# Pooled attention and a mixture of four experts on one core: another head, folds spread over slots, scores on row halves

## The chip, the cores and the metric

The kernel runs on one core of a Trainium2 chip. The core has a matrix engine (PE, TensorE) with its weight loads (PEld), a vector engine (DVE), a scalar engine (ACT), GpSimd (POOL) and a queue engine (SP). Each takes its own instructions in the order of the program; they wait for each other through semaphores. Loads are issued by POOL (queue q0 in the profile, "software_dynamic") or by SP (q1, "hardware_dynamic") and run on 16 DMA engines. The metric is the device time of one launch in microseconds (us); less is better.

## The reference

```python
k_p = k.reshape(B, H, Sp, 8, D).mean(axis=3)          # B, H, S, D = 8, 8, 576, 64; Sp = 72
v_p = v.reshape(B, H, Sp, 8, D).mean(axis=3)
scores = q @ k_p.T / 8                                 # per batch and head: 576 x 72
attn = softmax(scores)
x = (attn @ v_p), heads side by side                   # 4608 tokens x 512
p = domain_probs / domain_probs.sum(-1)                # 4608 x 4
out = sum over e of p[:, e] * (relu(x @ w1[e]) @ w2[e])  # w1: 512 x 1024, w2: 1024 x 512, e = 0..3
```

Keys and values are means over 8 neighbouring tokens, so each head has 72 keys. Inputs and output are float32; the kernel's products are in bfloat16.

## The kernel before

**Tiles.** The 4608 tokens are 36 tiles of 128, in 9 groups of 4 (512 tokens). A batch has 576 tokens, so tiles 4, 13, 22 and 31 lie over two batches and do their attention in two halves of 64 tokens. A step `s` is one group with one expert, 36 steps in all. `up` computes 128 of the 1024 hidden units for a whole group: 4 products of 128x128 weights with 512 columns, then relu on ACT. `down` takes one tile through w2 in 8 products of 512 columns; `collect` scales the result by the tile's probability and adds it up on DVE; the last expert's sum is stored. Up and down products, 2272 of 512 columns, are most of the work of PE.

**Attention of a tile.** `turn_q` transposes the queries (128 x 512) into `qT`; `scores` multiplies them with `kT`, the transposed key sums; `less_max` takes the maximum off on DVE; `expo` is on ACT; `turn_e` transposes the exponents; `context` multiplies with `vblk`, the value sums spread into blocks per head; `divide` is on DVE; `turn_x` transposes the result into `xT`, which `up` reads. In `kpad` each key sum stands in the columns of its head's parity, the other 64 columns being zero through `mask_k`; one product of 128 rows thus gives the scores of a pair of heads (144 columns). For tiles 0 to 7 the transpositions are products with an identity followed by a copy; from tile 8 on (`DT`) they are DMA transpositions issued by SP.

**Sums of keys and values.** `prep_k` and `prep_v` fold the 8 tokens of a mean on DVE, 4 + 2 + 1, all at once in the place where they are called; `kraw` and `vraw` have two buffers each, so the load of batch b + 2 waits for the folds of batch b.

**The head** (lines 516 to 567) computes group 0 with expert 0, tile by tile, before the regular steps start. The keys of batch 0 (`k0`, float32) come through SP in two parts of 256 rows and one of 64, the queries of the first 512 tokens through POOL as one load (`qg`), which DVE copies out tile by tile (`split_q`).

**The regular steps.** Each step has 12 slots. Two slots of three hold one `up` of the *next* step, the third a `down` and `collect` of this one. `plan` attaches the attention's functions to slots by number: step s, slot i is s * 12 + i. `plan_tile` sets a tile's order by `lead`, `late` and `last`, the slots between turned queries and scores, exponents and context, and transposed result and first use. A tile's `load_q` for the tile four later stands one slot behind `turn_q`. `plan_batch` places a batch's folds and the loads of the batch after next. Engines run their instructions in the order in which these calls are made: a slot's own product first, then what the plan has put there, in the order of planning.

**The loads** are issued by POOL in program order, at most eight under way, each issue behind the landing of the one eight before. The weights of all experts (16.8 MB in float32) come in the first 64 us, between queries, keys and values.

## Time and profile before

| | us |
|---|---|
| median of three runs (573.11 to 574.27) | 573.2 |
| the profiled execution | 575.8 |
| its span | 574.1 |
| PE busy | 541.6 |
| DVE / ACT / POOL busy | 259.8 / 209.3 / 62.8 |
| first full-width up product starts | 48.35 |
| one up (4 x 512 columns) / one down (8 x 512) | 0.86 / 1.73 |

The profile is of one execution. Its lines give an engine, an operation, the tiles that it writes and reads, how often, its busy time, and the idle time ahead of it with what ended that. Matmuls are pipelined: a single product lasts longer (379 ns for 512 columns) than the distance to the next one (216 ns). The granted clock is the share of TensorE's full clock that its throttle let through.

### The profile page before, as it was taken

The numbers are of one execution on the slowest core, as the hardware profiler recorded it, in microseconds if no ns is written. First come the engines' busy times: TensorE is split into PE (matmuls) and PEld (weight loads), VectorE is DVE, ScalarE is ACT, GpSimd is POOL, SyncE is SP. The second block draws the span as 40 slices with busy tenths as digits, with TensorE's granted clock in tenths as the row PEclk, the third lists the DMA queues.
The fourth block names the chain that finished last, engine by engine and source line by source line (L and its number), as shares of the span: only waits on it lengthen the run. The fifth ranks groups of instructions, "written<-read, shape, count | busy, mean of one in ns | idle before, by whom it ended". The sixth has DMA issues, their size and how long they took to land.

```text
span 574.1 us, 7199 instructions
## 1 busy us (share of the span) xinstructions
PE 541.6 (94%) x2906; PEld 263.1 (46%) x2906; DVE 259.8 (45%) x441; ACT 209.3 (36%) x352; POOL 62.8 (11%) x90
## 2 busy tenths in 40 slices
PE   1689997999999999899999999999999999999997
PEld 1554443444444444444444444444444444444443
DVE  4534675444733447344644445544553344322223
ACT  1345453333333333333333333333333333333330
POOL 7233313000310002200130000000000000000000
PEclk9799998999999999999999999999999999999999
DMA  9999999321692116911792244312311221111002
GB/s 198 206 203 197 203 148 89 86 48 31 96 159 50 30 31 110 149 25 31 110 159 36 39 77 87 39 30 65 77 29 29 59 75 31 21 34 49 1 0 74
DMA packets 111233, 46.03 MB, mean 80 GB/s; under 512 B 88128, under 2 KB 105984, under 8 KB 111200
## 3 DMA queue, kind: packets, MB, share of 16 engines
q0 software_dynamic: 51888, 21.96, 32.3%
q1 hardware_dynamic: 59312, 23.62, 18.4%
q8 instruction: 23, 0.38, 0.3%
q14 instruction: 10, 0.08, 0.1%
HBM read 45.16 MB, written 9.44 MB: 95 GB/s over the span
## 4 chain that ended last, share of the span: by engine, by line
PE 89%; DMA 4%; DVE 4%; ACT 2%; issue 1%; SPq 0%; DVEq 0%
PE o_ps L439 41%; PE h_ps L407 40%; DMA eT<-ebuf 3%; PE x_ps L372 3%; PE sc L302 2%; PE h_ps L422 2%; DMA k<-in_k_dram 1%; DVE xr L381 1%; DVE acc L454 1%; PE xT_ps L286 1%; ACT xT L287 0%; DVE mx L313 0%; DVE d_sb L315 0%; DVE vblk L260 0%; PE v_ps L272 0%
## 5 line engine op out<-in xcount | busy, mean ns | idle before, releaser
L411 ACT ACTIVATE h_sb<-h_ps 128x512 bf16<-128x512 f32 x280 | 167.2, 597 | 308.2 <-PE h_ps L407 308.1
L439 PE MATMUL o_ps<-w,h_sb 128*128 128x512 bf16 x1152 | 274.3, 381 | 0.0
L407 PE MATMUL h_ps<-xT,w 128*128 128x512 bf16 x1120 | 265.0, 379 | 0.7 <-ACT xT L287 0.7
L454 DVE SCALAR_TENSOR_TENSOR acc<-o_ps,p_sb,acc 128x512 f32<-128x512 f32 x108 | 81.1, 751 | 210.2 <-PE o_ps L439 210.2
L439 PEld LDWEIGHTS <-h_sb 128*128 128x128 bf16 x1152 | 112.2, 98 | 133.3 <-issue 1.9
L407 PEld LDWEIGHTS <-w 128*128 128x128 bf16 x1120 | 108.0, 98 | 124.1 <-issue 1.5
L450 DVE TENSOR_SCALAR acc<-o_ps,p_sb 128x512 f32<-128x512 f32 x36 | 27.0, 751 | 70.4 <-PE o_ps L439 70.4
L109 POOL DMA_DIRECT2D qrow<-in_q_dram x36 | 30.4, 865 | 77.1 <-DMA qT<-qrow 66.7
L313 DVE TENSOR_REDUCE mx<-sc 128x8 f32<-128x576 f32 x36 | 27.0, 749 | 5.5 <-PE sc L302 5.5
L315 DVE TENSOR_TENSOR d_sb<-sc,mx 128x576 f32<-128x576 f32 x36 | 27.3, 758 | 1.4
L321 ACT ACTIVATE ebuf<-d_sb 128x576 bf16<-128x576 f32 x36 | 24.4, 678 | 4.2 <-DVE d_sb L315 4.2
L381 DVE TENSOR_TENSOR xr<-x_ps,rs 128x512 bf16<-128x512 f32 x36 | 24.6, 683 | 2.8 <-PE x_ps L372 2.7
L339 DVE TENSOR_REDUCE total<-ebuf 128x8 f32<-128x576 bf16 x32 | 23.8, 743 | 0.8 <-ACT ebuf L321 0.8
L372 PE MATMUL x_ps<-vblk,eT 128*128 128x192 bf16 (+5 forms) x200 | 20.4, 242 | 4.0 <-DMA eT<-ebuf 2.1
L82 POOL DMA_DIRECT2D kraw<-in_k_dram x7 | 5.3, 756 | 163.8 <-DVE k_sum L232 160.6
L372 PEld LDWEIGHTS <-eT 128*128 128x128 bf16 (+1 forms) x200 | 14.4, 100 | 14.8 <-ACT eT L287 3.5
L302 PE MATMUL sc<-kT,qT 128*128 128x144 bf16 (+1 forms) x160 | 15.8, 234 | 3.8 <-ACT qT L287 2.5
L302 PEld LDWEIGHTS <-qT 128*128 128x128 bf16 (+1 forms) x160 | 10.8, 102 | 7.3 <-ACT qT L287 4.8
L255 PE MATMUL kT_ps<-ident,kpad 128*128 128x128 bf16 x10 | 1.2, 264 | 11.7 <-DVE kpad L241 11.7
L82 POOL DMA_DIRECT2D vraw<-in_v_dram x8 | 6.2, 771 | 43.9 <-DVE v_sum L232 37.2
L286 PE MATMUL xT_ps<-ident,xr 128*128 128x128 bf16 x32 | 3.4, 232 | 7.4 <-DVE xr L381 7.4
L422 PE MATMUL h_ps<-xT,w 128*128 128x128 bf16 x128 | 9.5, 243 | 0.5 <-ACT xT L287 0.5
(61 smaller groups left out, 135.8 us busy)
## 6 DMA issues: line engine op xcount, KB each, us to landing
out_dram<-acc SPq DMA_DIRECT2D x36, 256.0 KB, 2.2
vraw<-in_v_dram POOLq DMA_DIRECT2D x8, 512.0 KB, 8.2
w<-in_moe_w_dram POOLq DMA_DIRECT2D x8, 512.0 KB, 16.7
w<-in_moe_w_dram POOLq DMA_DIRECT2D x4, 1024.0 KB, 17.3
kraw<-in_k_dram POOLq DMA_DIRECT2D x7, 512.0 KB, 6.9
qrow<-in_q_dram POOLq DMA_DIRECT2D x28, 128.0 KB, 9.3
k<-in_k_dram SPq DMA_DIRECT2D x2, 512.0 KB, 4.0
qg<-in_q_dram POOLq DMA_DIRECT2D x1, 512.0 KB, 9.1
```

The source lines that it names most:

```text
L109: nc.gpsimd.dma_start(out=qrow[t][at:at + n], in_=q[b][:, tok:tok + n, :].rearrange("h p d -> p h d"),)
L302: nc.tensor.matmul(sc[at:at + n, pair // 2, (pair % 2) * PW:(pair % 2 + 1) * PW], lhsT=qT[t][:, pair, at:at + n], rhs=flat[:, pair * PW:(p ...
L313: nc.vector.reduce_max(out=mx[:], in_=view, axis=AX.X)
L315: nc.vector.tensor_tensor(out=ds[t][:], in0=view, in1=mx[:].unsqueeze(3).to_broadcast([P, 2, 4, SP]), op=ALU.subtract,)
L321: nc.scalar.activation(out=ebuf[t % 2][:, 0:ROWS].rearrange("p (h j) -> p h j", j=SP), in_=ds.pop(t)[:].rearrange("p g h j -> p (g h) j"), ...
L372: nc.tensor.matmul(ps[at:at + n, (2 * i - 1 + z0) * D:(2 * i - 1 + z1) * D], lhsT=eT[t][:, i, at:at + n], rhs=vblk[b][:, i, z0:z1].rearran ...
L381: nc.vector.tensor_tensor(out=rows_x[t][:], in0=xps.pop(t)[:].rearrange("p (h d) -> p h d", d=D), in1=es.pop(t)[:].unsqueeze(2).to_broadca ...
L407: nc.tensor.matmul(ps[:], lhsT=w1_sb[e][:, kc, fb * P:(fb + 1) * P], rhs=xT[g][:, kc, :], start=(kc == 0), stop=(kc == KC - 1),)
L411: nc.scalar.activation(out=hs[s][:, fb, :], in_=ps[:], func=ACT.Relu)
L439: nc.tensor.matmul(ps[:], lhsT=hs[s][:, fb, i * P:(i + 1) * P], rhs=w2_sb[e][:, fb, :], start=(fb == 0), stop=(fb == FB - 1),)
L450: nc.vector.tensor_scalar_mul(out=accs[t][:], in0=ps[:], scalar1=p_sb[:, e, t:t + 1])
L454: nc.vector.scalar_tensor_tensor(out=accs[t][:], in0=ps[:], scalar=p_sb[:, e, t:t + 1], in1=accs[t][:], op0=ALU.mult, op1=ALU.add,)
```

## The change

The keys are laid out as 96 rows x 6 instead of 128 x 5 with a short last part. `last_k` writes each key sum twice, side by side, with no mask, so both halves of `kT`'s rows hold all keys; `scores` does one product a head with 64 rows, even heads on the upper half, odd heads on the lower, 72 columns each, into two banks. `k0` comes in three equal parts, each folded as it lands, and is transposed in two pieces. `qg` comes in two loads and is transposed straight from there. In the head, products of zeros (`warm`) fill waits of PE at the start, zero fills are done by ACT, and the four tiles' work is interleaved in another order. In the regular steps the folds of a batch are spread over three or four slots, those of keys and values apart; `late` is 11 instead of 9; a tile is begun two slots earlier (`base`). The loads of the batch after next follow each fold, so load_k(3) is now issued at slot 11 and load_v(3) at slot 16, where both were at slot 15; load_q(8) stays at slot 14, and the scores of tile 8 move from slot 29 to 27. The folds of batch 2 move from slots 23 (keys) and 29 (values) to 30 to 32 and 42 to 45.

```diff
-    PW = 2 * SP
+    KP = 96
+    KB = ROWS // KP
...
-    kraw = [raw.tile([P, NB, POOL * D], BF16, name=f"kraw{i}") for i in range(2)]
+    kraw = [raw.tile([KP, KB, POOL * D], BF16, name=f"kraw{i}") for i in range(2)]
...
     def load_k(b):
-        load_rows(nc.gpsimd, kraw[b % 2], k[b])
+        nc.gpsimd.dma_start(
+            out=kraw[b % 2][:], in_=rows_of(k[b]).rearrange("(i p) x -> p i x", p=KP)
+        )
...
-    k0 = raw.tile([P, NB, POOL * D], F32, name="k0")
-    load_rows(nc.sync, k0, k[0], ((0, 2), (2, 4)))
+    KPARTS = ((0, 2), (2, 4), (4, KB))
+    k0 = raw.tile([KP, KB, POOL * D], F32, name="k0")
+    for i0, i1 in KPARTS:
+        nc.sync.dma_start(
+            out=k0[:, i0:i1, :],
+            in_=rows_of(k[0])[i0 * KP:i1 * KP].rearrange("(i p) x -> p i x", p=KP),
+        )
...
-    qg = raw.tile([P, H, TPG, D], BF16, name="qg")
-    nc.gpsimd.dma_start(
-        out=qg[:], in_=q[0][:, 0:G, :].rearrange("h (p c) d -> p h c d", c=TPG)
-    )
+    qg = [raw.tile([P, H, 2, D], BF16, name=f"qg{i}") for i in range(2)]
...
+    def load_qg(i):
+        nc.gpsimd.dma_start(
+            out=qg[i][:],
+            in_=q[0][:, 0:G, :].rearrange("h (p c) d -> p h c d", c=TPG)[
+                :, :, 2 * i:2 * i + 2
+            ],
+        )
+
+    zero = const.tile([P, 2 * P], BF16, name="zero")
+    nc.vector.memset(zero[:], 0.0)
+    load_qg(0)
+    ident = const.tile([P, P], BF16, name="ident")
+    make_identity(nc, ident[:])
+    load_v(0)
...
-    ident = const.tile([P, P], BF16, name="ident")
-    make_identity(nc, ident[:])
-    load_v(0)
-    load_w1(0)
+    load_w1(0, (0,))
+    load_qg(1)
+    load_w1(0, (1,))
...
-    nc.vector.memset(k0[TAIL:P, NB - 1, :], 0.0)
-    for t in (*kraw, *vraw):
-        nc.vector.memset(t[TAIL:P, NB - 1, :], 0.0)
+    for t in vraw:
+        nc.scalar.memzero(t[TAIL:P, NB - 1, :])
     for t in ebuf:
-        nc.vector.memset(t[:, ROWS:NB * P], 0.0)
+        nc.scalar.memzero(t[:, ROWS:NB * P])
...
-    mask_k = const.tile([P, NB, 2, D], BF16, name="mask_k")
...
-    def last_fold(rows, nm):
-        s = prep.tile([P, NB, D], BF16, name=f"{nm}_sum")
-        nc.vector.tensor_add(out=s[:], in0=rows[:, :, 0:D], in1=rows[:, :, D:2 * D])
-        return s
-
-    def prep_k(b, rows=None, parts=((0, NB),)):
-        rows = kraw[b % 2] if rows is None else rows
-        for i0, i1 in parts:
-            fold(rows, i0, i1, 4, 2)
-        s = last_fold(rows, "k")
-        pad = prep.tile([P, NB, 2, D], BF16, name="kpad")
-        nc.vector.tensor_tensor(
-            out=pad[:], in0=s[:].unsqueeze(2).to_broadcast([P, NB, 2, D]),
-            in1=mask_k[:], op=ALU.mult,
-        )
-        pads[b] = pad
-
-    def prep_kT(b, by_dma=True):
-        kT[b] = prep.tile([P, NB, P], BF16, name="kT")
+    def last_k(b, rows, i0, i1):
+        if i0 == 0:
+            pads[b] = prep.tile([KP, KB, 2, D], BF16, name="kpad")
+        shape = [KP, i1 - i0, 2, D]
+        nc.vector.tensor_add(
+            out=pads[b][:, i0:i1],
+            in0=rows[:, i0:i1, 0:D].unsqueeze(2).to_broadcast(shape),
+            in1=rows[:, i0:i1, D:2 * D].unsqueeze(2).to_broadcast(shape),
+        )
+    def fold_k(b, n):
+        fold(kraw[b % 2], 0, KB, n)
+    def end_k(b):
+        last_k(b, kraw[b % 2], 0, KB)
+    def kT_tile(b):
+        kT[b] = prep.tile([P, KB, KP], BF16, name="kT")
+        return pads[b][:].rearrange("p i z d -> p (i z d)")
+    def turn_k(b):
+        flat = kT_tile(b)
+        nc.sync.dma_start_transpose(out=kT[b][:], in_=flat)
+    def turn_k_by_products(b, i0, i1, pool, tag):
+        if i0 == 0:
+            kT_tile(b)
         flat = pads[b][:].rearrange("p i z d -> p (i z d)")
-        if by_dma:
-            nc.sync.dma_start_transpose(out=kT[b][:], in_=flat)
-            return
-        ps = ps_t.tile([P, NB, P], BF16, tag="t", name="kT_ps")
-        for i in range(NB):
-            nc.tensor.transpose(ps[:, i, :], flat[:, i * P:(i + 1) * P], ident[:])
-        nc.scalar.copy(out=kT[b][:], in_=ps[:])
-
-    def spread_v(b, s):
+        ps = pool.tile([P, i1 - i0, KP], BF16, tag=tag, name="kT_ps")
+        for i in range(i0, i1):
+            nc.tensor.transpose(
+                ps[:, i - i0, :], flat[:, i * P:(i + 1) * P], ident[0:KP, 0:KP]
+            )
+        nc.scalar.copy(out=kT[b][:, i0:i1, :], in_=ps[:])
...
+    def fold_v(b, n):
+        fold(vraw[b % 2], 0, NB, n)
+    def end_v(b):
+        rows = vraw[b % 2]
+        vsum[b] = prep.tile([P, NB, D], BF16, name="v_sum")
+        nc.vector.tensor_add(
+            out=vsum[b][:], in0=rows[:, :, 0:D], in1=rows[:, :, D:2 * D]
+        )
+    def spread_v(b):
         vblk[b] = prep.tile([P, NB, NZ, D], BF16, name="vblk")
         nc.vector.tensor_tensor(
-            out=vblk[b][:], in0=s.unsqueeze(2).to_broadcast([P, NB, NZ, D]),
+            out=vblk[b][:], in0=vsum[b][:].unsqueeze(2).to_broadcast([P, NB, NZ, D]),
             in1=mask_v[:], op=ALU.mult,
         )
 
-    def prep_v(b):
-        fold(vraw[b % 2], 0, NB, 4, 2)
-        spread_v(b, last_fold(vraw[b % 2], "v")[:])
-
-    def prep_v_by_products(b):
-        ps = ps_t.tile([P, NB, D], F32, tag="t", name="v_ps")
+    def sum_v_by_products(b):
+        ps = ps_o.tile([P, NB, D], F32, tag="o", name="v_ps")
         for r in range(POOL):
             nc.tensor.matmul(
                 ps[:], lhsT=ident[:], rhs=vraw[b % 2][:, :, r * D:(r + 1) * D],
                 start=(r == 0), stop=(r == POOL - 1),
             )
-        spread_v(b, ps[:])
+        vsum[b] = prep.tile([P, NB, D], BF16, name="v_sum")
+        nc.scalar.copy(out=vsum[b][:], in_=ps[:])
...
+        if t < TPG:
+            ps = ps_t.tile([P, NPAIR, P], BF16, tag="t", name="qT_ps")
+            for h in range(H):
+                nc.tensor.transpose(
+                    ps[(h % 2) * D:(h % 2 + 1) * D, h // 2, :],
+                    qg[t // 2][:, h, t % 2, :], ident[:],
+                )
+            (copy or nc.scalar.copy)(out=qT[t][:], in_=ps[:])
+            return
...
-            for pair in range(NPAIR):
+            for h in range(H):
+                half = slice((h % 2) * D, (h % 2 + 1) * D)
                 nc.tensor.matmul(
-                    sc[at:at + n, pair // 2, (pair % 2) * PW:(pair % 2 + 1) * PW],
-                    lhsT=qT[t][:, pair, at:at + n],
-                    rhs=flat[:, pair * PW:(pair + 1) * PW],
+                    sc[at:at + n, h % 2, (h // 2) * SP:(h // 2 + 1) * SP],
+                    lhsT=qT[t][half, h // 2, at:at + n],
+                    rhs=flat[half, h * SP:(h + 1) * SP],
...
-    def plan_batch(b, slot):
-        at(slot, prep_k, b)
-        at(slot + 2, prep_kT, b, b > 1)
-        at(slot + 6, prep_v, b)
+    def plan_k(b, slot, turn):
+        at(slot, fold_k, b, 4)
+        at(slot + 1, fold_k, b, 2)
+        at(slot + 2, end_k, b)
         if b + 2 < B:
-            at(slot + 6, load_k, b + 2)
-            at(slot + 6, load_v, b + 2)
+            at(slot + 2, load_k, b + 2)
+        at(slot + 2, *turn)
+
+    def plan_v(b, slot):
+        at(slot, fold_v, b, 4)
+        at(slot + 1, fold_v, b, 2)
+        at(slot + 2, end_v, b)
+        if b + 2 < B:
+            at(slot + 2, load_v, b + 2)
+        at(slot + 3, spread_v, b)
 
     def plan_tile(t, base):
         by_dma = t >= DT
-        lead, late, last = (10, 9, 6) if by_dma else (3, 3, 2)
+        lead, late, last = (10, 11, 6) if by_dma else (3, 3, 2)
...
-    plan_batch(1, SLOTS - 3)
+    plan_k(1, SLOTS - 3, (turn_k_by_products, 1, 0, KB, ps_t, "t"))
+    plan_v(1, SLOTS + 2)
     for i in range(TPG):
         assert plan_tile(TPG + i, SLOTS + 4 * i + 1) <= 3 * SLOTS + 1
     done_batches = 2
         for i in range(TPG):
             t = g * TPG + i
             due = (E * g - 1) * SLOTS - (TPG - 1 - i) * SLOTS
-            base = due - 29
-            last_b = ((t + 1) * P - 1) // S
-            if last_b >= done_batches:
-                plan_batch(last_b, base - 8)
+            base = due - 31
+            b = ((t + 1) * P - 1) // S
+            if b >= done_batches:
+                plan_k(b, base + (1 if b == 2 else -4), (turn_k, b))
+                plan_v(b, base + 13)
...
+    def warm(n):
+        ps = ps_h.tile([P, 2 * P], F32, tag="h", name="warm_ps")
+        for _ in range(n):
+            nc.tensor.matmul(ps[:], lhsT=zero[:, 0:P], rhs=zero[:])
+    def copy_v(out, in_):
+        nc.vector.tensor_copy(out=out, in_=in_)
+    warm(18)
+    for i0, i1 in KPARTS:
+        fold(k0, i0, i1, 4, 2)
+        last_k(0, k0, i0, i1)
+    turn_k_by_products(0, 0, 4, ps_o, "o")
+    warm(4)
+    turn_k_by_products(0, 4, KB, ps_o, "o")
+    spread_mask()
     turn_q(0)
-    split_q(1)
     scores(0)
     turn_q(1)
     less_max(0)
     expo(0)
     scores(1)
-    prep_v_by_products(0)
     less_max(1)
+    sum_v_by_products(0)
     turn_e(0)
     expo(1)
+    spread_v(0)
+    sums_by_products(0)
     context(0)
-    sums_by_products(0)
     divide(0)
-    split_q(2)
+    turn_e(1)
     turn_x(0)
-    turn_q(2)
+    turn_q(2, copy_v)
+    turn_q(3)
     scores(2)
-    up_tile(0, 0)
-    for t in range(TPG):
-        n = t + 1
-        if n + 1 < TPG:
-            less_max(n + 1)
-        if n < TPG:
-            turn_e(n)
-        if n + 1 < TPG:
-            expo(n + 1)
-        if t == 0:
-            domain_first()
-        if n < TPG:
-            down(0, t, 0, 3)
-            context(n)
-            sums_by_products(n)
-            divide(n)
-            down(0, t, 3, 6)
-            turn_x(n)
-            if n + 2 < TPG:
-                split_q(n + 2)
-                turn_q(n + 2)
-                scores(n + 2)
-            down(0, t, 6, FB)
-            up_tile(0, n)
-            collect(0, t)
+    less_max(2)
+    up_tile(0, 0, (0,))
+    expo(2)
+    sums_by_products(1)
+    context(1)
+    divide(1)
+    up_tile(0, 0, (1,))
+    turn_e(2)
+    turn_x(1, copy_v)
+    scores(3)
+    less_max(3)
+    up_tile(0, 1, (0,))
+    expo(3)
+    sums_by_products(2)
+    context(2)
+    divide(2)
+    up_tile(0, 1, (1,))
+    turn_e(3)
+    turn_x(2, copy_v)
+    domain_first()
+    up_tile(0, 2, (0,))
+    sums_by_products(3)
+    context(3)
+    divide(3)
+    up_tile(0, 2, (1,))
+    down(0, 0)
+    collect(0, 0)
+    turn_x(3)
+    down(0, 1)
+    collect(0, 1)
+    up_tile(0, 3)
+    down(0, 2)
+    collect(0, 2)
```

## The prediction

> **What bounds the kernel now.** The page comes first: TensorE (PE) is busy almost everywhere, so only the time in which it is not, or runs at a lower clock, can be won. Its second part says where that is.
>
> ```profile
> PE 541.6 (94%) x2906; PEld 263.1 (46%) x2906; DVE 259.8 (45%) x441; ACT 209.3 (36%) x352; POOL 62.8 (11%) x90
> PE   1689997999999999899999999999999999999997
> PEclk9799998999999999999999999999999999999999
> DMA  9999999321692116911792244312311221111002
> ```
>
> PE is short of work in the first three slices (43 us) and a little in the seventh. The DMA line matters as much: it is full for the first six slices, to about 80 us. The stretches before and after 48.35 us, where the first full-width up product starts, say the same; then the waits of PE behind it.
>
> ```profile
> 0.00:48.35 48.35, 27.11 (x273) 0.93 1.21 202
> 48.35:100.00 51.65, 46.62 (x285) 0.97 1.32 157
> 100.00:570.20 470.20, 467.91 (x2353) 1.00 0.35 59
> PE xT_ps L286 <- DVE xr L381: 4.0, 2, 2.8
> PE x_ps L372 <- DMA eT<-ebuf: 2.1, 2, 1.6
> PE h_ps L407 <- ACT xT L287: 0.7, 1, 0.7
> ```
>
> (Columns of the first three: length, PE busy, granted clock, DMA share, GB/s.) Behind 100 us PE idles 2.3 us in 470. So there is a head with 21 us of idle PE, a stretch to 100 us with 5, and a tail that gives 2.3 at most. The largest single wait, in the PE timeline and the windows around it:
>
> ```profile
> 86.49 1.03 PE L407 MATMUL h_ps<-xT,w 128*128 128x512 bf16 x4
> 90.37 0.40 PE L286 MATMUL xT_ps<-ident,xr 128*128 128x128 bf16 x4 [2.85 <-DVE xr L381]
> 87.56:90.98 3.42, 0.61 (x10) 0.62 (x11) 3.31 (x6) 0.77 (x2) 1.83 (x3) 1.00 0.13 8
> 90.98:94.39 3.41, 3.41 (x11) 1.18 (x8) 0.37 (x2) 1.58 (x3) 3.41 (x5) 0.50 1.12 157
> ```
>
> PE waited 2.9 us for a division that stood behind one batch's folds of the values (2.5 us of DVE from 87.15), and the window after it ran at half clock.
>
> Last, the loads. The POOL queue's loads run first in, first out at 200 GB/s from 5 us on, whatever the engines do. What matters is the transposed queries of tile 8, the first tile turned by DMA.
>
> ```profile
> kraw<-in_k_dram POOLq DMA_DIRECT2D x1, 512.0 KB, 14.5
> qrow<-in_q_dram POOLq DMA_DIRECT2D x1, 128.0 KB, 14.5
> DMA packets 204, 0.20 MB, mean 202 GB/s; under 512 B 7, under 2 KB 204, under 8 KB 204
> qT<-qrow SPq DMA_TRANSPOSE x1, 7.7
> ```
>
> The queries of tile 8 were issued at 55.72 and landed 14.5 later, at 70.2. The keys of batch 3 stand right behind them (58.23 + 14.5 = 72.7; their last rows 58.98 + 14.1 = 73.1). The transposition was issued at 70.34 and took 7.7 us (median of all 28: 2.4), because loads were in front: 78.0. The scores of tile 8 started at 85.0, 7 us later: no wait before.
>
> **Part 1, the head.** Before, the last part of `k0` (128 KB) landed at 8.9 although the two 512 KB parts were there by 5.8, as the queries and the small loads then shared the engines. After that came 2.6 us of DVE (folds .96 + .56, sum .49, masked copy .49) and scores(0) at 13.65. After: three parts of 384 KB. q1 moved 400 GB/s from 2.5 to 5 us, so the third part ends near 5.5 and lands about 6.1 (bound above: 8.9, its row before). DVE takes .69 + .43 + .43 = 1.6 a part, so kpad is done near 8.8 against 11.6; scores(0) at about 10.3. The query copies on DVE (4 x .28) go; memsets and masks (some 3 us of DVE ahead of 4.4 or in the wait for `k0`) were free already; the zero fills go to ACT, which sat idle till 12.4. Then the order: before, each tile went through scores, exponents, context and transposition alone, with PE waiting 7.4 us on divisions and 2.5 on qT; after, two tiles are under way at once. Walking the new order with the rows (less_max .75 + .76, expo .68, copies .59 to .69, inverse .37, division .68, 16 products of 128 columns .95) gives up_tile(0,0) near 20.4 (before 25.1), one tile every 4.1 us, then 5.2 us of down products and 2 of up_tile(0,3): the first full up product at 38.6, not 48.35. With the clock at half as in the old head (32 products took 3.6 us against 1.95) it is about 41. So 7 to 10 us are gained *there*.
>
> **Part 2, who is late next.** The loads do not come earlier: the bytes ahead of tile 8's queries are the same. And one step is moved against them. load_k(3) now stands at slot 11 (folds at 9, 10, 11), ahead of load_q(8) at slot 14; before it was at slot 15, behind it. POOL issues in order and the loads run in order, so tile 8's queries land 2.9 us later (70.2 + 2.9), and .3 more because `qg` comes in two loads with twice the pieces: 73.4. At the same time scores(8) moves from slot 29 to 27. The transposition ahead of it: bound below 2.4 (no load in front), above 9.6 (the slowest eT row); its own row is 7.7. I take 5.9, to 79.3: in both versions it is ready before load_v(3) ends (same total of bytes; issued 64.34, 11.5 to landing, so 75.9), and before it landed 2.1 us behind that, so 78.3 is the earliest I expect and 81.1 the full row.
> PE would reach scores(8) near 73 with the new head, and waits for some 6 us. Compared at equal work: before, scores(8) stood behind up(3,3) .86, scores(7) .25 and down(2,1) 1.73 that now come after it, so the old kernel was level at 85.0 - 2.84 = 82.2. Gain at this point: 82.2 - 79.3 = **2.9 us**, and all that the head won beyond it is lost. Waits of PE before that point (.4, 1.1) count for nothing any more. The new wait idles PE for more than one 3.4 us window, so the clock falls: as at 90.98, but from a random phase, so on average 4.6 us at half clock: **+2.3** (bounds 1.5 and 3.4).
>
> **Part 3, behind it.** The folds cost DVE what they did (2.1 us a batch for keys: .94 + .56 + .56 against .81 + .49 + .33 + .49), beside PE; but one a slot, and the division is no longer behind them: **-2.9**, and its half-clock window **-1.8** (8 products at 427 instead of 216 ns). The wait for xT (.7) stays, as the plan of tiles 4 to 7 is the same. eT gets 11 slots instead of 9, over 2 us more against waits of 1.6 and .5: **-2.1**. New small waits: the keys of batch 2 are finished at slot 32 and used at 39 (8.5 us of PE) with load_k(4) in the same slot, where transpositions took 6.8 to 7.5; and xT of tile 11, due 6 slots after it is issued, now meets load_k(5): together **+1.0** (0 to 3). POOL has fewer issues (one a batch of keys); it waits for landings anyway.
>
> **Part 4, the scores.** Four products of 128 x 144 become eight of 64 rows x 72 columns. No row has 64-row weights; the nearest is a tile over two batches, whose products use 64-column weights in pairs.
>
> ```profile
> 149.44 0.55 PE L372 MATMUL x_ps<-vblk,eT 128*128 128x192 bf16 x5
> 149.83 0.41 PE L302 MATMUL sc<-kT,qT 128*128 128x144 bf16 x4
> 150.08 0.38 PE L407 MATMUL h_ps<-xT,w 128*128 128x512 bf16 x1
> 163.89 0.55 PE L372 MATMUL x_ps<-vblk,eT 128*128 128x192 bf16 x5
> 164.37 0.45 PE L302 MATMUL sc<-kT,qT 128*64 128x144 bf16 x8
> 164.76 0.60 PE L407 MATMUL h_ps<-xT,w 128*128 128x512 bf16 x2
> ```
>
> Context and scores took .39 + .25 full, .48 + .39 in halves: +.23 for changing the shape of the array and back, while the pairs streamed 4 x 144 columns as before. Now the pairs stream 4 x 72, .125 less: +.105 a tile if they overlap as there, +.23 if they do not; -.125 if the change of shape were free. I take +.13, near the row's own behaviour. 25 tiles behind the wait (three halved ones stay): **+3.3** (2.6 to 5.8).
>
> **Sum.** -2.9 + 2.3 - 2.9 - 1.8 - 2.1 + 1.0 + 3.3 = -3.1 us. The profiled execution took 575.8 (span 574.1 and 1.7 around it), 2.6 above the median of 573.2. Part of that is likely the half-clock window, which hangs on phase; then 1.8 of the gain is not in the median. Between 573.2 - 3.1 = 570.1 and 571.9 I take **571.0**.
>
> **Rivals.**
> *The transposition gets in early.* If it took 2.4 us, as where no load is in front, or the 3.9 of one xT at the end of a load (223.85 us), scores(8) would start at 75.8 to 77.3 and the time be 567.5 to 569; with the short clock loss and the cheap halves 566. Against it: every transposition issued into a load that had just begun took 6.8 to 9.6. Chance .15. The Trainium skill (DMA: Bandwidth & Descriptors, section "Queues, rings and completion order") states that an engine turns to the next row of queues after a packet of typically 9 to 17 descriptors. The engines ran 204 packets in 1 us on 16 engines, 78 ns each, so by that rule the turn comes within 1.4 us (an estimate) and this rival is what happens; the 7.7 us above speaks for longer turns.
> *The row halves are dear (slower).* Eight weight loads instead of four: if pairs do not overlap (+.23) or each of the eight costs what one 144-column product did (62 ns: +.44 a tile), 25 tiles cost 5.8 to 11 us, and the time is 573.5 to 579. It decides from +.22 a tile on. Against it: the sums' products of 3 columns follow each other every 26 ns, weights included. The skill (TensorE: Matmul & The Clock Gate, section "LDWEIGHTS (loading the stationary operand)") gives P / 1.2 ns, 107 for 128 columns, estimated 20 us slower in all; the 26 ns speak against it here. Chance .2.
> *The transposition is as slow as its rows at worst.* 7.7 to 9.6 behind 73.4 lands at 81.1 to 83, level with before: 572.8 to 575. Chance .12. That it is hidden after all (PE not there before 79 because the head gained under 4 us) gives the forecast's time too, since the landing sets it.
>
> **How the numbers follow.** The forecast, 568.5 to 573.5: .53. Faster by over 0.2% (1.15 us, about what these runs tell from no change), below 572.05: .43 of that and .15: .58. Within: .08 of the forecast's, .06 of the slow transposition, .02 of the scores': .16. Slower: .18 of the scores', .06 of the slow transposition, .02 of the forecast's: .26. Range: from 566 (early landing, cheap halves) to 577 (dear halves, short of their worst).
>
> **What the profile after would show.** Right: first full up product near 39 to 41; a PE wait of 4 to 8 us at `sc` for the DMA of qT, ending at 78.5 to 81, with a window at about .5 behind it; DMA line full to 80 us as before; no wait for `xr` at 87, none for `eT` behind 200; scores with about .38 us from first product to the next line's, changes of shape included. Wrong: no such wait at `sc` (loads earlier than I worked out), the wait ending past 83, or scores over .5 us.

## The result, and the profile after

The changed kernel took 577.26 us (median of 13 runs, 575.25 to 579.38), the kernel before 575.3 beside it (13 runs, 573.11 to 576.85): a ratio of 1.0042, 95% interval 1.0025 to 1.0059. It is 2.4 us *slower*, where 571.0 against 573.2 was forecast, 2.2 faster. (573.2 was the median of three runs; over 13 runs the same kernel stands at 575.3, so it is the difference that can be compared, not 571.0 itself.) The profiled execution took 578.38 (span 576.7), 2.6 more than that of before. The page of it first: busy time of the engines, then PE, the granted clock and the DMA engines in 40 slices of 14.4 us.

```profile
PE 546.0 (95%) x3049; PEld 262.0 (45%) x3106; DVE 257.0 (45%) x428; ACT 212.1 (37%) x355; POOL 59.2 (10%) x84
PE   5998949999799999999999999999999999999997
PEclk7699969999989999999999999999999999999999
DMA  9999995662929112971399224212311131101001
```

The head is filled as intended: the first three slices of PE read 5, 9, 9 where they were 1, 6, 8. But the sixth slice (72 to 87 us) has a 4 and a clock of 6, and the eleventh (144 to 159) a 7, with a clock of 8 in the twelfth. Neither was there before. The list of PE's waits names both, with total, count and longest:

```profile
PE sc L345 <- DMA qT<-qrow: 7.3, 1, 7.3
PE kT_ps L277 <- DVE kpad L251: 5.2, 4, 1.5
PE h_ps L450 <- DMA xT<-xr: 4.1, 1, 4.1
```

The first and the third line are each one long wait for a DMA transposition; the second is four short ones, the longest 1.5 us. The wait for `xr` at 87 us and those for `eT` behind 200 are gone. PE's timeline around the two (start, length, group, and in brackets the idle time ahead of it):

```profile
73.88 0.44 PE L319 MATMUL eT_ps<-ident,ebuf 128*128 128x128 bf16 x5
81.66 0.42 PE L345 MATMUL sc<-kT,qT 64*128 64x72 bf16 x8 [7.34 <-DMA qT<-qrow]
...
153.01 1.89 PE L482 MATMUL o_ps<-w,h_sb 128*128 128x512 bf16 x7
159.00 3.35 PE L450 MATMUL h_ps<-xT,w 128*128 128x512 bf16 x8 [4.10 <-DMA xT<-xr]
```

And what SP and POOL had issued for them, from the timelines of all engines:

```profile
74.47 8.83 SPq L335 DMA_TRANSPOSE qT<-qrow  x2
...
147.01 1.20 SPq L269 DMA_TRANSPOSE kT<-kpad  x1
147.28 0.74 POOL L84 DMA_DIRECT2D kraw<-in_k_dram  x1 [34.99 <-DVE kpad L251]
148.00 1.78 POOL L111 DMA_DIRECT2D qrow<-in_q_dram  x2
148.39 1.21 SPq L335 DMA_TRANSPOSE qT<-qrow  x1
149.65 2.00 SPq L436 DMA_TRANSPOSE xT<-xr  x1
```

Tile 8's transposition was issued at 74.47 and PE went on at 81.66, 7.2 us later; the `xT` of tile 11 was issued at 149.65 and used at 159.00, 9.4 later. PE would have wanted it at 154.90, so it had 5.2. Beside it ran the load of batch 5's keys, issued at 147.28, and two of queries. The windows around both waits (length, busy PE, PEld, DVE, ACT, POOL, then granted clock, DMA share, GB/s):

```profile
73.23:76.64 3.41, 0.89 (x10) 0.51 (x9) 1.39 (x4) 1.77 (x3) 1.37 (x2) 1.00 1.79 179
76.64:80.05 3.41, 0.00 (x0) 0.00 (x0) 0.00 (x0) 0.00 (x0) 0.00 (x0) 0.50 2.84 145
80.05:83.47 3.42, 1.81 (x12) 0.69 (x12) 1.31 (x2) 0.00 (x0) 0.00 (x0) 0.50 0.31 26
83.47:86.88 3.41, 3.19 (x16) 1.29 (x16) 1.72 (x3) 1.17 (x2) 0.00 (x0) 0.50 0.33 63
86.88:90.29 3.41, 3.41 (x26) 1.87 (x25) 2.28 (x5) 1.91 (x4) 0.00 (x0) 1.00 0.08 15
155.15:158.56 3.41, 0.00 (x0) 0.00 (x0) 0.54 (x1) 0.00 (x0) 0.00 (x0) 1.00 1.48 125
158.56:161.97 3.41, 2.97 (x8) 1.04 (x9) 0.00 (x0) 0.60 (x1) 0.00 (x0) 0.50 0.41 39
161.97:165.38 3.41, 3.41 (x32) 1.52 (x30) 0.83 (x2) 0.99 (x2) 0.00 (x0) 1.00 0.00 0
```

A window in which PE was mostly idle (busy 0.89 of 3.41 us) or all idle is followed by one at half clock. There the clock stayed behind a window with 1.81 us busy, and came back behind 3.19 and behind 2.97. The first wait so costs another 2.6 us (5.2 us of half clock behind 81.66), the second 1.5 (8 up products take 3.19 us from 159.00 to 162.19, where 8 take 1.73 elsewhere). The Trainium skill (TensorE: Matmul & The Clock Gate, Part 1) has the clock halve after an idle window of about 3.4 us and return after a busy one. These rows agree on the return; the fall came sooner here, at 76.64, when PE had been idle for only 2.3 us (from 74.32).

### The profile page after: what moved, and what is told of

Its sections match the earlier page's. It is cut to its first block, busy times and chain, and to the rows that moved or that the text cites. A ratio compares the mean times of both kernels' runs of the same rounds, so it can differ in the third digit from the quotient of the medians.

```text
span 576.7 us, 7523 instructions
## 1 busy us (share of the span) xinstructions
PE 546.0 (95%) x3049; PEld 262.0 (45%) x3106; DVE 257.0 (45%) x428; ACT 212.1 (37%) x355; POOL 59.2 (10%) x84
## 4 chain that ended last, share of the span: by engine, by line
PE 90%; DMA 4%; DVE 2%; another core or an unknown queue 1%; issue 1%; ACT 1%; SPq 0%
PE o_ps L482 42%; PE h_ps L450 41%; PE x_ps L415 3%; PE sc L345 2%; DMA xT<-xr 2%; PE h_ps L465 2%; DMA qT<-qrow 1%; DMA k<-in_k_dram 1%; PE v_ps L304 0%; PE xT_ps L319 0%; PE eT_ps L319 0%; ACT xT L320 0%; DVE acc L493 0%; DVE kraw L241 0%
## 5 line engine op out<-in xcount | busy, mean ns | idle before, releaser
L450 PE MATMUL h_ps<-xT,w 128*128 128x512 bf16 x1088 | 268.9, 382 | 6.1 <-DMA xT<-xr 4.1
L482 PE MATMUL o_ps<-w,h_sb 128*128 128x512 bf16 x1127 | 270.6, 380 | 1.6 <-issue 0.4
L497 DVE SCALAR_TENSOR_TENSOR acc<-o_ps,p_sb,acc 128x512 f32<-128x512 f32 x108 | 81.1, 751 | 210.6 <-PE o_ps L482 208.2
L450 PEld LDWEIGHTS <-w 128*128 128x128 bf16 x1120 | 106.4, 98 | 125.4 <-DMA xT<-xr 4.6
L345 PE MATMUL sc<-kT,qT 64*128 64x72 bf16 (+1 forms) x320 | 11.7, 205 | 9.8 <-DMA qT<-qrow 7.3
L345 PEld LDWEIGHTS <-qT 64*128 64x128 bf16 (+1 forms) x320 | 7.0, 101 | 23.6 <-issue 12.3
L241 DVE TENSOR_TENSOR kraw<-kraw 96x1536 bf16<-96x1536 bf16 (+1 forms) x14 | 10.3, 738 | 0.0
L465 PEld LDWEIGHTS <-w 128*128 128x128 bf16 x128 | 9.0, 109 | 1.3 <-issue 0.9
```

The source lines that it names most:

```text
L345: nc.tensor.matmul(sc[at:at + n, h % 2, (h // 2) * SP:(h // 2 + 1) * SP], lhsT=qT[t][half, h // 2, at:at + n], rhs=flat[half, h * SP:(h + ...
L450: nc.tensor.matmul(ps[:], lhsT=w1_sb[e][:, kc, fb * P:(fb + 1) * P], rhs=xT[g][:, kc, :], start=(kc == 0), stop=(kc == KC - 1),)
L465: nc.tensor.matmul(ps[:, f], lhsT=w1_sb[e][:, kc, (f0 + f) * P:(f0 + f + 1) * P], rhs=xT[g][:, kc, cols], start=(kc == 0), stop=(kc == KC ...
L482: nc.tensor.matmul(ps[:], lhsT=hs[s][:, fb, i * P:(i + 1) * P], rhs=w2_sb[e][:, fb, :], start=(fb == 0), stop=(fb == FB - 1),)
L497: nc.vector.scalar_tensor_tensor(out=accs[t][:], in0=ps[:], scalar=p_sb[:, e, t:t + 1], in1=accs[t][:], op0=ALU.mult, op1=ALU.add,)
```

## The experiments

Each kernel was timed beside the kernel before, whose median was 575.38 (runs 1 to 4), 575.16 (5 to 8) and 576.2 (9 to 12); ratios are to it, with 95% intervals. "By the ratios" below means the difference to 1.0042, in parts of 575.3 us.

**1. The keys of batch 5, later.** Only the place of one load on the POOL queue changes; PE, ACT and SP have the same instructions in the same order.

```diff
-            at(slot + 2, load_k, b + 2)
+            at(slot + (20 if b == 3 else 2), load_k, b + 2)
```

> The changed kernel, with the load of batch 5's keys put behind that of batch 5's values on the POOL queue. Theory A (the load beside which xT of tile 11 is turned is what makes PE wait 4.1 us at 154.5, and that wait pulls the clock down for one window): the wait of h_ps for DMA xT goes, the window at half clock from 158.6 goes with it, and the time falls by 4.1 + 1.7 = 5.8 us, to a ratio of about 0.994 to the kernel before. Theory B (xT of tile 11 is late for its own reasons, its turn behind those of kT and qT on the same queue): the wait stays at 2 us or more, the time falls by 2 or less. A wait that opens elsewhere, where the keys now land (about 180 to 187 us), would show there.

Measured: 571.14 us, 0.9927 (0.9901 to 0.9953): 6.6 us less than the changed kernel by the ratios, 6.1 by the medians. PE's timeline where the wait had been, and SP's:

```profile
150.63 1.89 PE L450 MATMUL h_ps<-xT,w 128*128 128x512 bf16 x8
152.36 1.89 PE L482 MATMUL o_ps<-w,h_sb 128*128 128x512 bf16 x7
154.08 1.89 PE L450 MATMUL h_ps<-xT,w 128*128 128x512 bf16 x8
```

```profile
148.97 1.26 SPq L436 DMA_TRANSPOSE xT<-xr  x1
```

The transposition, at the same place behind those of kT and qT, is now in time, and the clock stays at 1.00 from 85.93 on. So theory A: the load made `xT` late. No wait opened where the keys now land. This one load costs more than the whole loss of 2.4 us.

**2. The keys of batch 3, back behind tile 8's queries.**

```diff
-            at(slot + 2, load_k, b + 2)
+            at(slot + (6 if b == 1 else 2), load_k, b + 2)
```

> The changed kernel, with the load of batch 3's keys put back behind tile 8's queries, as before the change. Theory A (the step that moved the load ahead of the queries cost 2.9 us at the first scores of tile 8): the queries land at 71.5 instead of 74.4, the transposition still takes 7 us behind running loads, the wait at sc ends near 78.7 instead of 81.7, the time falls by 2.5 to 3.5 us, ratio about 1.000 to the kernel before. Theory B (the transposition ends when the run of loads ends, at 82 us, whenever it is issued): the wait ends where it did, the time stays (ratio 1.004).

Measured: 575.28 us, 0.9994 (0.9973 to 1.0015), 2.8 less by the ratios, 2.0 by the medians. The transposition's issue and the end of the wait, from SP's and PE's timelines:

```profile
71.20 8.97 SPq L335 DMA_TRANSPOSE qT<-qrow  x2
```

```profile
78.53 0.42 PE L345 MATMUL sc<-kT,qT 64*128 64x72 bf16 x8 [5.25 <-DMA qT<-qrow]
```

Issued 3.3 us earlier, it is done 3.1 us earlier, after 7.3 us: it does not wait for the loads to end at 82 us (theory B). The order of the two loads is what the prediction said it is.

**3. Tile 8's queries turned by products.**

```diff
-        if t >= DT:
+        if t > DT:
             nc.sync.dma_start_transpose(out=qT[t][:], in_=flat)
...
-        at(base, turn_q, t)
+        if t == DT:
+            lead, late = lead + 1, late - 1
+        at(base + (10 if t == DT else 0), turn_q, t)
```

> The changed kernel, with the queries of tile 8 turned by four products just before its scores, which come one slot later, instead of by a DMA. Theory A (what the new head won is lost waiting for this one transposition): no wait for a DMA at sc, the first products of tile 8 near 75 instead of 81.7, no window at half clock behind it; the time falls by 7.3 of wait and 2.6 of clock, less 0.3 for the products and up to 1 for the queries' landing at 74.4: 8.5 to 9.6 us, ratio about 0.989 to the kernel before. Theory B (the loads are the limit of the whole stretch, so that the next transposition, eT of tile 8, qT of tile 9 or kT of batch 2, takes the wait over): the time falls by 4 us or less, and a wait for one of these stands in the list.

Measured: 571.23 us, 0.9925 (0.9896 to 0.9955), 6.7 us less by the ratios, 6.0 by the medians: between the two. The long wait is gone, and two small ones stand in its place:

```profile
73.38 0.40 PE L319 MATMUL qT_ps<-ident,qrow 128*128 128x128 bf16 x4 [2.11 <-DMA qrow<-in_q_dram]
...
76.73 0.42 PE L345 MATMUL sc<-kT,qT 64*128 64x72 bf16 x8 [1.74 <-DVE d_sb L358]
```

The first is the landing of the queries themselves. The second is of my edit: tile 8's scores came right ahead of tile 7's, which need the same tile of PSUM (`sc`, one buffer) and wait for DVE. With them the clock is at 0.50 from 74.58 to 81.40: PE was busy 1.30 us in the window ahead of that and 1.45 in the first window of it. None of theory B's three waits appears.

**4. The scores on row halves, alone, in the kernel before.**

```diff
-            for pair in range(NPAIR):
+            for h in range(H):
+                half = slice((h % 2) * D, (h % 2 + 1) * D)
                 nc.tensor.matmul(
-                    sc[at:at + n, pair // 2, (pair % 2) * PW:(pair % 2 + 1) * PW],
-                    lhsT=qT[t][:, pair, at:at + n],
-                    rhs=flat[:, pair * PW:(pair + 1) * PW],
+                    sc[at:at + n, h % 2, (h // 2) * SP:(h // 2 + 1) * SP],
+                    lhsT=qT[t][half, h // 2, at:at + n],
+                    rhs=flat[half, h * SP:(h + 1) * SP],
                 )
```

> The kernel before, with the scores per head on row halves alone, and the two heads of a pair in two banks of PSUM, as the change has them; the folds, the head and the plan as they were. Theory A (changes of the array's shape in and out, +0.13 us a tile, 32 tiles with DMA or late turning): slower by 3.3 to 4.2 us, ratio 1.006 to 1.007. Rival (eight products of 64 rows cost +0.23 or more): slower by 6 us or more, ratio over 1.010. Rival (free): within 1 us.

Measured: 576.56 us, 1.0014 (0.9997 to 1.0031): 0.8 us by the ratio, at most 1.8 by the interval. So theory A's 3.3 to 4.2 is excluded, and the rival "free" (within 1 us) is not. The rows of the trace are finer. A whole tile and one over two batches, in PE's timeline:

```profile
150.68 0.55 PE L373 MATMUL x_ps<-vblk,eT 128*128 128x192 bf16 x5
151.16 0.30 PE L303 MATMUL sc<-kT,qT 64*128 64x72 bf16 x8
151.39 0.82 PE L408 MATMUL h_ps<-xT,w 128*128 128x512 bf16 x3
...
165.22 0.55 PE L373 MATMUL x_ps<-vblk,eT 128*128 128x192 bf16 x5
165.70 0.34 PE L303 MATMUL sc<-kT,qT 64*64 64x72 bf16 x16
165.97 0.82 PE L408 MATMUL h_ps<-xT,w 128*128 128x512 bf16 x2
```

Context and scores of a whole tile take 0.48 + 0.23 = 0.71 against 0.64 before: +0.07, not +0.13. A tile over two batches, whose scores had changed the array's shape before too, takes 0.75 against 0.87. So 32 tiles at +0.07 and 4 at -0.12, +1.8 us, the upper end of what was measured. The Trainium skill (TensorEngine Tiling (Array Packing), Key Properties) says that a change of the tiling mode drains TensorE, and (Theoretical Speedup) that a product of 64 rows gains up to two times. These rows agree with the first: between context and scores 0.09 us is added where the shape now changes. Of the second they show 0.39 to 0.27 us for the scores where the shape was changed before, and 0.25 to 0.23 where it was not. There the change of shape eats the gain.

**5. Both waits at once** (the edits of 1 and 3).

> The changed kernel with both earlier edits together: the keys of batch 5 behind the values of batch 5, and tile 8's queries turned by four products. Theory A (two separate waits, each with its own window at half clock): the two gains add, 6.1 + 6.0 = 12 us off the changed kernel, ratio about 0.982 to the kernel before. Theory B (they hang together, the stretch gained at tile 8 meets the same loads later): 9 us or less, ratio 0.987 or more.

Measured: 566.24 us, 0.9849 (0.9819 to 0.9879), 11.1 us less by the ratios. Alone they gave 6.6 and 6.7 (6.1 and 6.0 by the medians), together 11.1 (11.0): nearer to theory A's 12 than to B's 9, and 1 to 2 short of the sum, which the intervals allow. Neither wait is in its list any more; that something is lost between them is not shown, and not excluded.

**6. Tile 8's queries loaded ahead of expert 3's weights**, turned by DMA, with the edit of 1.

```diff
     load_q(TPG + 2)
+    load_q(DT)
     load_w1(3)
...
-        if t + TPG < NT:
+        if t + TPG < NT and t + TPG != DT:
             at(base + 1, load_q, t + TPG)
...
-        qT[t] = soft.tile([P, NPAIR, P], BF16, name="qT")
+        qT[t] = qtp.tile([P, NPAIR, P], BF16, name="qT")
```

(`qtp` is a pool with three buffers.)

> The changed kernel with the keys of batch 5 late, and with tile 8's queries loaded ahead of expert 3's weights instead of behind the keys of batch 3, turned by DMA as in the change, with a third buffer for the turned queries. Theory A (the wait is a matter of where the load stands in the row of loads): the queries land near 55 instead of 74.4, the transposition, 7 to 10 us in running loads, is done before 66, and PE goes through scores of tile 8 near 74 with no wait and no window at half clock: 6.1 + 7.3 + 2.6 = 16 us off the changed kernel, ratio about 0.975. Theory B (the transposition can't get in until the loads end near 82): the wait stays, ratio as with the keys late alone, 0.993.

Measured: 562.83 us, 0.979 (0.9763 to 0.9818), 14.5 us less than the changed kernel by the ratios, 14.4 by the medians, for one moved load and one buffer more. Theory A's ratio of 0.975 lies just outside the interval, theory B's 0.993 far outside. PE where it had waited 7.3 us:

```profile
73.97 0.30 PE L347 MATMUL sc<-kT,qT 64*128 64x72 bf16 x8
74.20 1.04 PE L452 MATMUL h_ps<-xT,w 128*128 128x512 bf16 x4
76.06 0.30 PE L347 MATMUL sc<-kT,qT 64*128 64x72 bf16 x8 [0.82 <-DVE d_sb L360]
```

The transposition itself took 8.8 us among the loads (issued at 53.78); it only has time for it. The third buffer belongs to the edit; what the moved load gives without it was not run.

**7. The new plan alone, in the kernel before**, with the two loads where they do no harm. The folds become `fold_k`, `end_k`, `fold_v`, `end_v` over the old layout; the head stays.

```diff
-        at(slot, prep_k, b)
-        at(slot + 2, prep_kT, b, b > 1)
-        at(slot + 6, prep_v, b)
+        at(slot, fold_k, b, 4)
+        at(slot + 1, fold_k, b, 2)
+        at(slot + 2, end_k, b)
         if b + 2 < B:
-            at(slot + 6, load_k, b + 2)
-            at(slot + 6, load_v, b + 2)
+            at(slot + {1: 6, 3: 20}.get(b, 2), load_k, b + 2)
...
-        lead, late, last = (10, 9, 6) if by_dma else (3, 3, 2)
+        lead, late, last = (10, 11, 6) if by_dma else (3, 3, 2)
...
-            base = due - 29
+            base = due - 31
```

> The kernel before with the plan of the change alone: folds in pieces, one a slot, eT with 11 slots, each tile two slots earlier; batch 3's keys stay behind tile 8's queries and batch 5's keys go behind batch 5's values, so that neither of the two waits can come from the loads. The head, the masks and the scores in pairs are those of before. By the prediction's terms the stall at 87 (2.9), its window at half clock (1.8) and the waits for eT (2.1) go: 5 to 6.8 us faster, ratio 0.988 to 0.991. Rival (the folds' stall only moves, to another division or to the late queries): within 2 us, ratio 0.997 or more.

Measured: 571.52 us, 0.9939 (0.9917 to 0.9961): 3.5 us faster, between the two. The stalls at 87 and behind 200 are gone, and the clock stays at 1.00 from 29.59 on, as theory A has it; but the list of waits has new ones:

```profile
PE kT_ps L269 <- DVE kpad L255: 13.9, 2, 12.3
...
PE sc L315 <- DVE d_sb L328: 2.1, 2, 1.3
```

Of the first, 12.3 are the old head's (11.7 in the profile before); 1.6 is new, since batch 1's keys are turned in the same slot as their last sum. The second line had 1.3 before; 0.8 is new, at the scores of tiles 8 and 7 in one slot after the other.

**8. The new head and scores with the old plan**: `plan_batch`, `late` 9 and `base = due - 29` of before put into the changed kernel.

```diff
-        at(slot + 2, end_k, b)
+        at(slot, end_k, b)
...
+        at(slot + 6, fold_v, b, 4)
...
         if b + 2 < B:
-            at(slot + 2, load_k, b + 2)
+            at(slot + 6, load_k, b + 2)
+            at(slot + 6, load_v, b + 2)
```

> The changed kernel with the plan of before: folds of a batch together in one slot, eT with 9 slots, the loads of keys and values together 6 slots behind the folds. What is left of the change is the head and the scores on row halves. Theory A (what the head wins is lost at the wait for tile 8's queries, which the loads set): about the kernel before, plus 1.4 for the scores, plus the clock behind the wait, less up to 3.7: ratio 0.998 to 1.003. Rival (the head's gain comes through): 7 us or more faster, ratio 0.988 or less.

Measured: 568.77 us, 0.9888 (0.9862 to 0.9913). *Here my theory fell*: the head's gain does come through, 6.4 us of it, the rival's figure all but reached. SP's and PE's timelines:

```profile
70.76 1.29 SPq L335 DMA_TRANSPOSE qT<-qrow  x1
```

```profile
76.72 0.38 PE L482 MATMUL o_ps<-w,h_sb 128*128 128x512 bf16 x1
78.37 0.30 PE L345 MATMUL sc<-kT,qT 64*128 64x72 bf16 x8 [1.28 <-DMA qT<-qrow]
```

The old plan's two waits for `xr` behind the folds are still there (2.3 and 2.5 us), and the time falls all the same. The profiled execution is the fastest of the five (567.07), with the first full-width up product at 37.56. Tile 8's transposition ends almost when it did in the kernel before (issued 70.34, 7.7 us: 78.0). But there PE reached those scores only at 85.0, so the loads left 7 us of room, and the new head takes 6.6 of them. The room is lost only with the new plan: it asks for the scores with 2.8 us of PE's work less in front of them, and gets them 3.3 us later (81.66 for 78.37), behind the keys of batch 3. That is 6.1 of the 6.6.

**9. Both loads of keys back** (the edits of 1 and 2).

> The changed kernel with both loads of keys where they stood in the kernel before: batch 3's behind tile 8's queries, batch 5's behind batch 5's values. Theory A (two loads, each moved into the way of one transposition, are all that the new plan costs): the gains of the two single edits add, 6.1 + 2.0 = 8.1 us off the changed kernel, which is where the new head with the old plan stood: 569.2 us, ratio 0.989. Theory B (the plan costs by something else too, the scores of tile 8 two slots earlier or the pieces): 571 us or more, ratio 0.993 or more.

Measured: 568.8 us, 0.9882 (0.9859 to 0.9906). The two gains add (9.2 us by the ratios), and the new plan then stands where the old one does under the new head. By the lists of waits it is no better because what it wins at the folds and at `eT` it pays at tile 8: here 6.1 for `qT` and 0.7 for `xr`, under the old plan (run 8) 1.3 for `qT`, 5.3 for `xr` and 0.3 for `eT`. Its line in run 9:

```profile
PE sc L345 <- DMA qT<-qrow: 6.1, 1, 6.1
```

**10 and 11. The products of zeros**, taken out of kernel 6 (22 fewer), and increased there to 46.

```diff
-    warm(18)
...
-    warm(4)
```

> The kernel with tile 8's queries early and the keys of batch 5 late (562.8 us), without the 22 products of zeros in the head. Theory A (they come too early to hold the clock: behind them PE is busy .9 of a 3.4 us window and the clock is at half to 25 us anyway): within 1 us, 561.8 to 563.8. Theory B (they are what keeps the clock up when the head starts): slower by 2 to 4 us, 564.8 to 566.8.

> The same kernel (562.8 us) with 46 products of zeros in place of 22, the new ones in the waits between 5 and 18 us. Theory A (the clock follows PE's busy share of the last window, and the head's work of 8 to 25 us runs at half only because PE idles): more of the head at full clock, up to 3 us faster, 559.8 to 561.8. Theory B (the zeros stand in front of the head's own products at half clock, or the granting is a matter of phase): 0 to 1.5 us slower, 562.8 to 564.3.

Measured: 562.66 us, 0.9775 (0.975 to 0.98) without; 563.5 us, 0.9788 (0.9762 to 0.9815) with more. Neither differs from kernel 6 (0.979). The first full-width up products, in PE's timelines of kernel 6, without zeros, and with more:

```profile
39.61 1.67 PE L452 MATMUL h_ps<-xT,w 128*128 128x512 bf16 x7
```

```profile
39.56 2.75 PE L452 MATMUL h_ps<-xT,w 128*128 128x512 bf16 x12
```

```profile
36.99 5.34 PE L452 MATMUL h_ps<-xT,w 128*128 128x512 bf16 x24
```

The 22 zeros change no time that these intervals show: theory A. With 46 the one profiled execution was 2.6 us ahead, with the clock up from 13.91 instead of 25.06; it was also the fastest of its six runs (561.17; slowest 564.27). But kernel 3, with 22 zeros, ran its head at full speed from about 17 us on in its profile (five context products in 0.55 us at 16.98, against 0.91 at 17.52 in kernel 6), and its first full-width product came at 36.85. Over the profiles with this head and 22 zeros that start lies between 36.85 and 39.89. So the head's clock differs from execution to execution, one profile each cannot tell the three kernels apart, and whether more zeros help stays open.

**12. Scores in pairs again for whole tiles from tile 9 on**, in kernel 6, with a mask on the keys of batches 2 and up.

```diff
+            if paired(t):
+                for c in range(NPAIR):
+                    nc.tensor.matmul(
+                        sc[at:at + n, c // 2, (c % 2) * 2 * SP:(c % 2 + 1) * 2 * SP],
+                        lhsT=qT[t][:, c, at:at + n],
+                        rhs=flat[:, c * 2 * SP:(c + 1) * 2 * SP],
+                    )
+                continue
             for h in range(H):
```

> The same kernel (562.8 us) with the scores of every whole tile from tile 9 on in pairs of heads again, as before the change, with keys masked by one product on DVE in the slot of their last sum; tiles over two batches stay on row halves. By the rows of the profiles a whole tile costs .33 us on row halves and .25 in pairs, 24 tiles: 2.0 us faster, 560.8. Rival (the mask's product on DVE delays a division or a transposition): no gain.

Measured: 561.91 us, 0.9751 (0.9725 to 0.9778): the fastest kernel here, 2.5% below the kernel before. Against kernel 6 it is 0.9 us by the medians and 2.2 by the ratios, with intervals that overlap, so the time alone does not prove it. The trace does show the saving at its place: behind 100 us a whole tile, from the four up products ahead of its scores to the next line, takes 0.86 + 0.25 us in pairs, and 0.96 + 0.24 on row halves in kernel 6 (medians). That is 0.09 a tile, some 2 us for 24 tiles.

## Why the prediction was wrong, point by point

**The failing step** is in Part 3: "New small waits: ... xT of tile 11, due 6 slots after it is issued, now meets load_k(5): together +1.0 (0 to 3)". The place and the mechanism were right, and the other wait in that term (for the keys of batch 2) did not come. The size was 4.1 us of wait and 1.5 of half clock, 5.6 in the profile and 6.1 to 6.6 by run 1. It could have been worked out: in the trace of before this transposition is issued at 151.02 and its first use, the first up product of group 2, starts at 156.99. That is 6.0 us of room. Transpositions in running loads took 6.8 to 9.6 us there, so this one would be late by 0.8 to 3.6, before any clock loss. (In the changed kernel the room was 5.2 and the time to use 9.4.) I priced it as a nuisance and never set its room against its rows, and none of my signs of being wrong named it. With that load moved the kernel is 4.2 us faster than the kernel before (0.9927), where 2.2 was forecast: the sign is right again, the size is not, and the closeness of 571.14 to the 571.0 forecast is luck, since the kernel before stood at 575.4 beside it and not at 573.2.

**Tile 8's scores, -2.9.** Right in kind, wrong in size: the wait ends at 81.66, not 79.3, so the gain over the old kernel's 82.2 is 0.5. The transposition was issued at 74.47 and not 73.4; with the loads in the same order the queries were there at 74.3 in run 1 and 73.4 in run 3, so 73.4 lies within what executions differ by. It took 7.2 and not the 5.9 that I took; its own row, 7.7, was nearer. In the eight kernels that turn these queries by DMA at 70 to 75 us, it took 6.9 to 7.7 from issue to landing, and none shows the shortening at the end of a load that I counted on. That the head's gain is lost there was true, but as a matter of the plan (run 8), not of the loads alone, as I had it.

**The clock behind it, +2.3.** 2.6. Right. (The clock fell after 2.3 us of idle, and not after a whole window.)

**The stall at 87 with its window, -2.9 and -1.8, and the waits for `eT`, -2.1.** All gone in the trace, as forecast. Run 7 gives 3.5 us for them (2.2 to 4.8 by its interval) and not 6.8; 2.4 us of waits come with the same plan (`kT_ps` 1.6, `sc` 0.8), which leaves 4.4, inside that interval. In the changed kernel the first lies ahead of tile 8's wait and costs nothing, and the second does not appear.

**The scores, +3.3 (2.6 to 5.8).** Some +1.3: 24 whole tiles behind tile 8 at 0.07, three over two batches at -0.12. Below my lower bound of 0.105 a tile: I had taken the price from the scores of a tile over two batches (0.39 us up to the next line's) and took off 0.125 for the shorter stream, which leaves 0.265; a whole tile's eight products took 0.23. And I let the tiles over two batches stay as they were, though they gain. The rival that they are dear is refuted by run 4.

**The head.** First full product at 39.89, forecast 38.6 to 41 (36.85 to 39.89 over the profiles with this head). The third part of `k0` was there at 8.1 and not 6.1, and the first scores came a us later than worked out (11.4 for 10.3).

**The sum**, in profiled executions: -0.5 + 2.6 - 2.9 - 1.8 - 2.1 + 5.6 + 1.3 = +2.2, against +2.6 measured. Two errors of some 2 us (tile 8, too good; scores, too dear) nearly cancel; the 4.6 us by which `xT` of tile 11 was under-priced decide the sign. The 1.1 us that I added for the median rested on three runs of before (573.2); over 13 runs the median is 575.3, only 0.5 below the profiled execution. The rival that the transposition is as slow as at worst was nearest (7.2 us behind 74.47, "lands at 81.1 to 83"), yet by itself it would have given no change.

**Misreadings that moved little.** Of the 7.4 us of waits for divisions that I put into the old head, 4.0 lie behind 48.4, as the list for that stretch says. The DMA line of before reads 9 in seven slices and not in six (the rate falls from 203 to 148 GB/s in the sixth). A window of 3.41 us at half clock can cost 1.7 and not 1.8. And +0.44 a tile for dear row halves does not come out of its rows: eight products at 62 ns are 0.50 us, 0.25 more than before, or 0.48 with 0.23 for the shape.

## What to carry to other kernels

A load that is moved has to be set against every transfer that it meets, not only the one it was moved past: for each, the room between issue and first use, against the slow rows of its kind, plus the clock window that a wait of a few us costs. And a gain at one stage reaches the end only up to the next thing whose time is fixed by something else; a plan that asks for that thing earlier spends the gain. Both were here a matter of two lines: with the same head, folds and scores, two loads placed otherwise give 568.8, and tile 8's queries ahead of a weight, with a third buffer for them, 562.8.

## What the runs showed of the hardware that was not expected

- A DMA transposition of 128 KB (tile 8's queries) beside running loads took 6.9 to 7.7 us from issue to landing in the eight kernels that issued it at 70 to 75 us, and 8.8 in run 6, which issued it at 53.78; the median of all transpositions of queries in the change is 2.4.
- On row halves, eight products of 64 rows with 72 columns are no dearer than four of 128 rows with 144 (0.23 for 0.25 us up to the next line's); only the 0.09 ahead of the first is added, and where the shape was changed before, 0.12 is won.
- Two short waits of 2.1 and 1.7 us, 1.6 us of work apart, came with two windows at half clock (74.58 to 81.40 in run 3), as many as a single idle of 6.1 us in run 9 (75.0 to 81.8). A wait need not fill a window: 1.30 us busy of 3.41 was followed by half clock, while 2.12 and 2.04 in run 8 (75.40 to 82.20) were not.
- The products of zeros ahead of the head (18 of them, 3.8 us from 1.1 us on, and 4 later) moved neither the first full product in the two profiles (39.61 with, 39.56 without) nor the time (562.83 and 562.66).
